# First loads and first products of a gated linear-attention and SwiGLU kernel: x tile 0 alone on one queue, x tile 1 on the other, two key products moved ahead of a transpose

## The chip, the cores and the metric

The kernel runs on one core of a Trainium2 chip. The time is device microseconds of one execution. Six runs of the kernel before gave a median of 179.36 us.

## The reference

All inputs are bf16. `x` is 2048 x 512, `wqkv` 512 x 1536, `wo` 512 x 512, `w1` and `w3` 512 x 1376, `w2` 1376 x 512, and `gate_w` has 512 entries. The attention has 32 heads of width 16.

```
qkv = x @ wqkv, split into q, k, v and 32 heads
phi(t) = where(t > 0, t + 1, exp(t)) + 1e-6
kv = sum over tokens of phi(k)^T v ;  z = sum over tokens of phi(k)
a = ((phi(q) kv) / (phi(q) . z + 1e-6)) @ wo
b = (silu(x @ w1) * (x @ w3)) @ w2
g = sigmoid(sum(x * gate_w))
out = g * a + (1 - g) * b
```

## The kernel before

**Tiles and stages.** The 2048 tokens are 16 tiles of 128 (`NT`), four tiles to a block of 512 (`NTB` = 4). The 512 features are four chunks of 128 (`KC`, index `kc`). The kernel has three stages. In the first it computes k for each token tile, applies phi, adds the results for z (`pks`, on GpSimd) and accumulates `XP`, which is x transposed times phi(k). In the second it turns `XP` into the matrix `W_sb`, while the gate and up products of the first block run. In the third it goes over the four blocks with the feed-forward products, the q products of the next block, and the output products. Everything is held in SBUF; each weight is loaded once.

**x in two layouts.** `XP` needs x with tokens on the partitions (`x_sb`). All other products need x with features on the partitions (`xT`). For tiles 2 to 15 `xT` comes by transposing DMAs (lines 87 and 91). For tiles 0 and 1 TensorE makes it: `emit_xT(t)` (line 170) issues four transposes of 128x128 from `x_sb` into two PSUM tiles `xTp`, two transposes to each. The first `xTp` (features 0 to 255, `kc` 0 and 1) is copied to `xT` by VectorE (line 180), the second (`kc` 2 and 3) by ScalarE (line 182). The two calls use four different PSUM buffers (tags XP0 to XP3).

**The loads and their queues.** Two engines issue DMAs: SyncE (queue SP, `dq` in the code) and, for one load only, ScalarE (queue ACT). Line 82 loads x tiles 0 and 1 together on SP; each partition takes two neighbouring tokens, which are 2 KB in one piece. Tile 0 is then the even tokens of the first 256 and tile 1 the odd ones, and the stores of output tiles 0 and 1 use the same pattern (`out_first`, lines 81 and 377). Line 83 loads the first half of the key weights (`wk_sb`, `kc` 0 and 1) on ACT, and line 84 the second half (`kc` 2 and 3) on SP. Behind them on SP come the transposing load of tiles 2 and 3 (line 87), the rest of x, and the other weights in the order of their use. The weights `w2` come in two halves (lines 110 and 111).

**The order on TensorE** is the program's own: `tc.manual_schedule` (line 151) fixes it, so that a matmul which waits holds up all that stands behind it. First come nine warm-up matmuls on constants (`emit_warm`, line 166: six of 512 columns, three of 128), which need no data. Then follow `emit_xT(0)`, `emit_xT(1)`, and the key products of lines 385 and 386: `kc` 0 and 1 of tile 0, `kc` 0 and 1 of tile 1, `kc` 2 and 3 of tile 0. Line 389 does the rest of tile 1, and then tiles 2 and 3. The key products `kc` 0 and 1 of a tile read the `xT` half that VectorE copied, and the first half of `wk_sb`. From tile 4 on, the key products (`k_ps`) alternate with the `XP` products (line 396).

**ScalarE at the start** issues the load of line 83, then loads the activation table and runs a one-element Exp (line 86), and is then free for the copies of line 182.

Of the kernel before, what the change touches and what calls it, by code (L numbers as in the profile page):

```python
# [17 lines left out]
def kernel(  # L18
# [12 lines left out]
    nc = tc.nc  # L31
    P = nc.NUM_PARTITIONS
# [7 lines left out]
    TB = 512  # L40
    NTB = S // TB
    TPB = TB // P
    FC = F // P
# [5 lines left out]
    x2d = A_x.flatten_outer_dims()  # L49
    out2d = out.flatten_outer_dims()  # L50
# [11 lines left out]
    x_sb = consts.tile([P, NT, D], BF16, name="x_sb")  # L62
# [7 lines left out]
    w2_sb = consts.tile([P, FC, D], BF16, name="w2_sb")  # L70
# [6 lines left out]
    x_r = x2d.rearrange("(t p) d -> p t d", p=P)  # L77
    dq = nc.sync
    TF = 2
    x_first = x2d[0 : TF * P, :].rearrange("(p j) d -> p j d", j=TF)  # L80
    out_first = out2d[0 : TF * P, :].rearrange("(p j) d -> j p d", j=TF)
    dq.dma_start(out=x_sb[:, 0:TF, :], in_=x_first)
    nc.scalar.dma_start(out=wk_sb[:, 0:2, :], in_=wqkv_r[:, 0:2, D : 2 * D])
    dq.dma_start(out=wk_sb[:, 2:4, :], in_=wqkv_r[:, 2:4, D : 2 * D])
    pre = consts.tile([1, 1], FP32, name="pre")
    nc.scalar.activation(out=pre[:], in_=nc.const_aps.tensor(0.0, [1, 1], FP32), func=ACT.Exp)
    dq.dma_start(
        out=xT[:, :, TF * P : TB], in_=x2d[TF * P : TB, :], transpose=True
    )
    for tb in range(1, NTB):  # L90
        dq.dma_start(
            out=xT[:, :, tb * TB : (tb + 1) * TB], in_=x2d[tb * TB : (tb + 1) * TB, :],
# [7 lines left out]
    with nc.allow_non_contiguous_dma(reason="one gate weight per partition and chunk"):  # L100
        dq.dma_start(
            out=wr_sb[:, :, 2 * FR : NR], in_=gate_w.rearrange("(kc d o) -> d kc o", d=P, o=1)
# [4 lines left out]
        dq.dma_start(out=w3_sb[:, :, fsl], in_=w3_r[:, :, fsl])  # L107
    dq.dma_start(out=wo_sb[:], in_=A_wo.rearrange("(kc d) n -> d kc n", d=P))
    w2_r = B_w2[0:FM, :].rearrange("(fc f) d -> f fc d", f=P)
    for fcs in (slice(0, FC // 2), slice(FC // 2, FC)):  # L110
        dq.dma_start(out=w2_sb[:, fcs, :], in_=w2_r[:, fcs, :])
    dq.dma_start(out=w2r_sb[:FR, :], in_=B_w2[FM:F, :])

    pk_sb = consts.tile([P, NT, D], BF16, name="pk_sb")
# [5 lines left out]
        out=bm, in_=bm, pattern=[[-Dh, HPC], [0, Dh]], compare_op=ALU.is_ge, fill=0.0,  # L120
# [3 lines left out]
        out=bm, in_=bm, pattern=[[Dh, HPC], [0, Dh]], compare_op=ALU.is_ge, fill=0.0,  # L124
# [34 lines left out]
    def emit_warm(*widths):  # L159
        warm = psX.tile([P, TB], FP32, tag="XP3", name="warm")  # L160
        for n in widths:
            nc.tensor.matmul(  # L162
                warm[:, 0:n], lhsT=warm_l, rhs=warm_r[:, 0:n], start=True, stop=True
            )

    emit_warm(TB, TB, TB, TB, TB, TB, P, P, P)

    st = {}

    def emit_xT(t):  # L170
        for h in range(2):
            xTp = psX.tile([P, 2, P], BF16, tag=f"XP{(2 * t + h) % 4}", name="xTp")
            for j in range(2):
                kc = 2 * h + j
                nc.tensor.transpose(  # L175
                    out=xTp[:, j, :], in_=x_sb[:, t, kc * P : (kc + 1) * P], identity=ident[:]
                )
            xT_t = xT[:, 2 * h : 2 * h + 2, t * P : (t + 1) * P]
            if h == 0:
                nc.vector.tensor_copy(out=xT_t, in_=xTp[:])  # L180
            else:
                nc.scalar.activation(out=xT_t, in_=xTp[:], func=ACT.Copy)

    def emit_k_mm(k_ps, t, kc):
        nc.tensor.matmul(  # L185
            k_ps[:], lhsT=xT[:, kc, t * P : (t + 1) * P], rhs=wk_sb[:, kc, :],
            start=(kc == 0), stop=(kc == KC - 1),
        )
# [148 lines left out]
    def emit_out(tb, tt):  # L337
        t = tb * TPB + tt
        tsl = slice(tt * P, (tt + 1) * P)

        if t < NT - 1:
            parts = [(0, D, True)]
        else:
            h, q7 = D // 2, 7 * D // 8
            parts = [(0, h, True), (h, q7, False), (q7, D, True)]
        if t < NT - 1:
            o_out = work.tile([P, D], BF16, tag="o_out", name="o_out")
        else:
            o_out = consts.tile([P, D], BF16, name="o_last")
        lo = 0  # L350
        for i, (a, b, store) in enumerate(parts):
            o_ps = psX.tile([P, b - a], FP32, tag=f"XP{2 + (tt + i) % 2}", name="o_ps")
            for c in range(KC):
                nc.tensor.matmul(  # L354
                    o_ps[:], lhsT=st[tb, "pqT"][:, c, tsl], rhs=W_sb[:, c, a:b],
                    start=(c == 0), stop=False,
                )
            nc.tensor.matmul(  # L358
                o_ps[:], lhsT=st[tb, "hTr"][:, tsl], rhs=w2r_sb[:, a:b],
                start=False, stop=False,  # L360
            )
            for fc in range(FC):
                nc.tensor.matmul(  # L363
                    o_ps[:], lhsT=st[tb, "hT"][:, fc, tsl], rhs=w2_sb[:, fc, a:b],
                    start=False, stop=(fc == FC - 1),
                )
            if i == 0:
                nc.scalar.activation(  # L368
                    out=o_out[:, a:b], in_=o_ps[:], func=ACT.Copy, scale=omg[:, t : t + 1]
                )  # L370
            else:
                nc.vector.tensor_scalar(  # L372
                    out=o_out[:, a:b], in0=o_ps[:], scalar1=omg[:, t : t + 1], scalar2=None,
                    op0=ALU.mult,
                )
            if store:
                rows = out_first[t] if t < TF else out2d[t * P : (t + 1) * P, :]
                nc.sync.dma_start(out=rows[:, lo:b], in_=o_out[:, lo:b])
                lo = b


    k0 = [psM.tile([P, D], FP32, tag="mm", name=f"k0_{t}") for t in range(TPB)]
    emit_xT(0)
    emit_xT(1)
    for kc, t in ((0, 0), (1, 0), (0, 1), (1, 1), (2, 0), (3, 0)):
        emit_k_mm(k0[t], t, kc)
    emit_k_phi(k0[0], 0)
    for t in range(1, TPB):
# [15 lines left out]
    with tc.manual_schedule(engines={ENG.DVE}):  # L404
# [18 lines left out]
        for dc in range(KC):  # L423
# [9 lines left out]
            out=z_sb[:].rearrange("p (b f) -> p b f", f=Q),  # L433
            in_=z_col[:, :, None].to_broadcast([P, NB, Q]),
        )
        kvT_ps = psX.tile([P, KC, P], FP32, tag="XP0", name="kvT_ps")
        for c in range(KC):
# [7 lines left out]
            out=kvT_sb[:], in0=kvT_ps[:],  # L445
# [22 lines left out]
    for tb in range(NTB):  # L468
        for fc in range(FC if tb == 0 else 0, FC):
            emit_ffn(tb, fc)  # L470
        nx = tb + 1
        for tt in range(TPB):
            if nx < NTB:
                emit_q(nx, tt, psX, "XP0")
                if tt % 2 == 0:
                    emit_rem(nx, tt // 2, psX, "XP1")
                    if tt == 2:
                        emit_omg(nx)
            emit_out(tb, tt)
            if nx < NTB:  # L480
                emit_den(nx, tt)
        if nx < NTB:
            emit_norm(nx)
# [30 lines left out]
```

## Time and profile before

| what | value |
|---|---|
| median of six runs (lowest, highest) | 179.36 us (178.57, 179.77) |
| the profiled execution, its own time | 179.77 us |
| its span, first to last instruction | 177.9 us |
| TensorE busy | 173.5 us, 98% of the span |
| VectorE, ScalarE, GpSimd busy | 119.1, 65.1, 63.8 us |
| x tiles 0 and 1 (256 KB): issued, time to landing | 0.81 us, 2.8 us |
| first half of wk (256 KB): issued, time to landing | 0.80 us, 3.5 us |
| second half of wk (256 KB): issued, time to landing | 1.27 us, 3.9 us |

All starts are counted from the first instruction of the span. The profiled execution is the longest of the six; 1.87 us of its time lie outside the span. A matmul's listed duration is longer than its distance to the next one, because matmuls overlap in the array; where the text speaks of the time that a matmul takes, it means the distance between starts.

### The profile page before, as it was taken

The numbers are of one execution on the slowest core, as the hardware profiler recorded it, in microseconds if no ns is written. First come the engines' busy times: TensorE is split into PE (matmuls) and PEld (weight loads), VectorE is DVE, ScalarE is ACT, GpSimd is POOL, SyncE is SP. The second block draws the span as 40 slices with busy tenths as digits, with TensorE's granted clock in tenths as the row PEclk, the third lists the DMA queues.
The fourth block names the chain that finished last, engine by engine and source line by source line (L and its number), as shares of the span: only waits on it lengthen the run. The fifth ranks groups of instructions, "written<-read, shape, count | busy, mean of one in ns | idle before, by whom it ended". The sixth has DMA issues, their size and how long they took to land.

```text
span 177.9 us, 2456 instructions
## 1 busy us (share of the span) xinstructions
PE 173.5 (98%) x867; PEld 84.2 (47%) x883; DVE 119.1 (67%) x205; ACT 65.1 (37%) x122; POOL 63.8 (36%) x80
## 2 busy tenths in 40 slices
PE   8999999999999999999999999999999999999993
PEld 4444444474444545444454544444545444444463
DVE  0398667899999837498786375978754669776001
ACT  3542423476532333342333333342433323331221
POOL 6087765689154323262003232620032328000000
PEclk9999999999999999999999999999999999999999
DMA  5999999901005011123000111240001012200002
GB/s 177 245 288 240 298 365 360 329 8 29 10 0 115 3 44 33 44 59 89 0 0 11 37 37 37 59 90 6 0 7 58 16 60 69 59 0 0 29 30 62
DMA packets 30252, 15.14 MB, mean 85 GB/s; under 512 B 20672, under 2 KB 30112, under 8 KB 30240
## 3 DMA queue, kind: packets, MB, share of 16 engines
q1 hardware_dynamic: 29968, 14.72, 30.2%
q10 hardware_dynamic: 272, 0.26, 0.5%
q8 instruction: 7, 0.11, 0.3%
q14 instruction: 5, 0.04, 0.1%
HBM read 8.42 MB, written 2.10 MB: 59 GB/s over the span
## 4 chain that ended last, share of the span: by engine, by line
PE 97%; issue 1%; DVE 0%
PE up_ps L321 19%; PE gate_ps L313 19%; PE o_ps L363 19%; PE XP L205 8%; PE o_ps L354 8%; PE q_ps L218 8%; PE k_ps L185 6%; PE r_ps L242 3%; PE k L185 2%; PE o_ps L358 2%; PE warm L162 2%; PE kvT_ps L440 1%; PE W_ps L458 0%; PE xTp L175 0%; DVE o_last L372 0%
## 5 line engine op out<-in xcount | busy, mean ns | idle before, releaser
L321 PE MATMUL up_ps<-xT,w_sb 128*128 128x512 bf16 x157 | 40.7, 379 | 0.2
L313 PE MATMUL gate_ps<-xT,w_sb 128*128 128x512 bf16 x157 | 40.7, 379 | 0.2
L226 POOL TENSOR_TENSOR qz<-pq,z_sb 128x512 f32<-128x512 bf16 x16 | 18.5, 1164 | 58.0 <-DVE pq L146 58.0
L326 ACT ACTIVATE th<-gate_ps 128x512 bf16<-128x512 f32 x40 | 23.9, 598 | 39.1 <-PE gate_ps L313 37.6
L363 PE MATMUL o_ps<-w_sb,hT 128*128 128x512 bf16 (+3 forms) x177 | 37.3, 355 | 0.2
L328 DVE SCALAR_TENSOR_TENSOR gs<-th,gate_ps 128x512 bf16<-128x512 bf16 x40 | 27.3, 682 | 5.4 <-ACT th L326 5.1
L333 DVE TENSOR_TENSOR hT<-up_ps,gs 128x512 bf16<-128x512 f32 x40 | 27.6, 691 | 3.8
L143 DVE TENSOR_SCALAR phi_m<-phi_e 128x512 bf16<-128x512 bf16 x32 | 13.6, 426 | 21.7 <-ACT phi_e L141 21.6
L363 PEld LDWEIGHTS <-hT 128*128 128x128 bf16 x180 | 16.9, 98 | 17.8
L321 PEld LDWEIGHTS <-w_sb 128*128 128x128 bf16 x160 | 15.7, 98 | 18.9
L313 PEld LDWEIGHTS <-w_sb 128*128 128x128 bf16 x160 | 15.6, 98 | 18.6
L293 POOL TENSOR_TENSOR pqn<-pq,rden 128x512 bf16<-128x512 bf16 x16 | 16.6, 1058 | 15.0 <-DVE rden L286 13.1
L368 ACT ACTIVATE o_out<-o_ps,omg 128x512 bf16<-128x512 f32 x15 | 10.3, 688 | 28.9 <-PE o_ps L363 28.9
L195 POOL TENSOR_TENSOR pks<-pks,pk_sb 128x512 f32<-128x512 f32 x15 | 17.4, 1162 | 7.3 <-DVE pk_sb L146 6.7
L354 PE MATMUL o_ps<-W_sb,pqT 128*128 128x512 bf16 (+3 forms) x70 | 16.7, 355 | 0.1
L205 PE MATMUL XP<-pk_sb,x_sb 128*128 128x512 bf16 x62 | 16.2, 379 | 0.1
L229 DVE TENSOR_REDUCE den<-qz 128x32 f32<-128x512 f32 x16 | 10.9, 684 | 7.9 <-POOL qz L226 7.8
L218 PE MATMUL q_ps<-wq_sb,xT 128*128 128x512 bf16 x61 | 16.1, 379 | 0.1
L141 ACT ACTIVATE phi_e<-k_ps 128x512 bf16<-128x512 f32 x12 | 7.2, 597 | 14.4 <-PE k_ps L185 14.4
L141 ACT ACTIVATE phi_e<-q_ps 128x512 bf16<-128x512 f32 x16 | 9.6, 597 | 7.8 <-PE q_ps L218 6.7
L185 PE MATMUL k_ps<-wk_sb,xT 128*128 128x512 bf16 x48 | 12.3, 379 | 0.0
L146 DVE SCALAR_TENSOR_TENSOR pq<-q_ps,phi_m 128x512 bf16<-128x512 f32 x16 | 11.1, 691 | 0.5
(60 smaller groups left out, 120.8 us busy)
## 6 DMA issues: line engine op xcount, KB each, us to landing
w_sb<-in_B_w_dram SPq DMA_DIRECT2D x6, 640.0 KB, 8.6
out_dram<-o_out SPq DMA_DIRECT2D x15, 128.0 KB, 1.9
x_sb<-in_A_x_dram SPq DMA_DIRECT2D x2, 512.0 KB, 4.2
x_sb<-in_A_x_dram SPq DMA_DIRECT2D x1, 768.0 KB, 5.1
wq_sb<-in_A_wqkv_dram SPq DMA_DIRECT2D x1, 512.0 KB, 4.9
wv_sb<-in_A_wqkv_dram SPq DMA_DIRECT2D x1, 512.0 KB, 6.4
wo_sb<-in_A_wo_dram SPq DMA_DIRECT2D x1, 512.0 KB, 10.2
wk_sb<-in_A_wqkv_dram ACTq DMA_DIRECT2D x1, 256.0 KB, 3.5
```

The costliest lines, as they stand in the source:

```text
L185: nc.tensor.matmul(k_ps[:], lhsT=xT[:, kc, t * P : (t + 1) * P], rhs=wk_sb[:, kc, :], start=(kc == 0), stop=(kc == KC - 1),)
L195: nc.gpsimd.tensor_add(pks[:], pks[:], pk_sb[:, t, :])
L205: nc.tensor.matmul(XP_ps[dc][:], lhsT=x_sb[:, t, dc * P : (dc + 1) * P], rhs=pk_sb[:, t, :], start=(t == 0), stop=(t == NT - 1),)
L218: nc.tensor.matmul(q_ps[:], lhsT=xT[:, kc, ts_tok], rhs=wq_sb[:, kc, :], start=(kc == 0), stop=(kc == KC - 1),)
L226: nc.gpsimd.tensor_tensor(out=qz[:], in0=st[tb, "pq"][:, tt, :], in1=z_sb[:], op=ALU.mult)
L313: nc.tensor.matmul(gate_ps[:], lhsT=w1_sb[:, kc, fsl], rhs=xT[:, kc, tok_sl], start=(kc == 0), stop=(kc == KC - 1),)
L321: nc.tensor.matmul(up_ps[:], lhsT=w3_sb[:, kc, fsl], rhs=xT[:, kc, tok_sl], start=(kc == 0), stop=(kc == KC - 1),)
L326: nc.scalar.activation(out=th[:], in_=gate_ps[:], func=ACT.Tanh, scale=0.5)
L328: nc.vector.scalar_tensor_tensor(out=gs[:], in0=th[:], scalar=1.0, in1=gate_ps[:], op0=ALU.add, op1=ALU.mult)
L333: nc.vector.tensor_tensor(out=st[tb, "hT"][:, fc, :], in0=up_ps[:], in1=gs[:], op=ALU.mult)
L354: nc.tensor.matmul(o_ps[:], lhsT=st[tb, "pqT"][:, c, tsl], rhs=W_sb[:, c, a:b], start=(c == 0), stop=False,)
L363: nc.tensor.matmul(o_ps[:], lhsT=st[tb, "hT"][:, fc, tsl], rhs=w2_sb[:, fc, a:b], start=False, stop=(fc == FC - 1),)
```

## The change

The load of x is split. Tile 0 goes first and alone on SP, in rows of 1 KB, with the plain token order. Tile 1 goes on ACT, behind the first half of wk. The stores of output tiles 0 and 1 use the plain order too. One of the six wide warm-up matmuls is taken out. The first two key products of tile 0 are issued between the transposes of tile 0 and those of tile 1. The two loads of `w2` become one.

```diff
-    x_first = x2d[0 : TF * P, :].rearrange("(p j) d -> p j d", j=TF)
-    out_first = out2d[0 : TF * P, :].rearrange("(p j) d -> j p d", j=TF)
-    dq.dma_start(out=x_sb[:, 0:TF, :], in_=x_first)
+    dq.dma_start(out=x_sb[:, 0, :], in_=x_r[:, 0, :])
     nc.scalar.dma_start(out=wk_sb[:, 0:2, :], in_=wqkv_r[:, 0:2, D : 2 * D])
+    nc.scalar.dma_start(out=x_sb[:, 1, :], in_=x_r[:, 1, :])
     dq.dma_start(out=wk_sb[:, 2:4, :], in_=wqkv_r[:, 2:4, D : 2 * D])
...
-    for fcs in (slice(0, FC // 2), slice(FC // 2, FC)):
-        dq.dma_start(out=w2_sb[:, fcs, :], in_=w2_r[:, fcs, :])
+    dq.dma_start(out=w2_sb[:], in_=w2_r)
...
-    emit_warm(TB, TB, TB, TB, TB, TB, P, P, P)
+    emit_warm(TB, TB, TB, TB, TB, P, P, P)
...
-                rows = out_first[t] if t < TF else out2d[t * P : (t + 1) * P, :]
+                rows = out2d[t * P : (t + 1) * P, :]
...
     emit_xT(0)
+    emit_k_mm(k0[0], 0, 0)
+    emit_k_mm(k0[0], 0, 1)
     emit_xT(1)
-    for kc, t in ((0, 0), (1, 0), (0, 1), (1, 1), (2, 0), (3, 0)):
+    for kc, t in ((0, 1), (1, 1), (2, 0), (3, 0)):
         emit_k_mm(k0[t], t, kc)
```

## The prediction, made before the changed kernel was run

> **What bounds the kernel now.** I read the page first, then the chain of work that ended last, the waits of TensorE, the order of time at the start, and the DMA queues in short stretches. The page and the waits of TensorE:
>
> ```profile
> span 177.9 us, 2456 instructions
> PE 173.5 (98%) x867; PEld 84.2 (47%) x883; DVE 119.1 (67%) x205; ACT 65.1 (37%) x122; POOL 63.8 (36%) x80
> PE 97%; issue 1%; DVE 0%
> ```
>
> ```profile
> PE warm L162 <- PEq L498: 0.8, 1, 0.8
> ```
>
> TensorE waits once, for 0.8 us, before its first instruction, and never again. So a delay of TensorE near the start has no later wait to vanish in: it reaches the end in full, and so does a gain. All that matters of this change is what it does to TensorE's stream in the first 7 us. The chain there (start, duration, what):
>
> ```profile
> 0.84 3.04 PE warm L162 x9
> 3.88 0.85 PE xTp L175 x8
> 4.74 4.43 PE k L185 x16
> 9.17 0.86 PE XP L205 x4
> ```
>
> and the same stretch in order of time (start, duration, engine, line):
>
> ```profile
> 3.63 0.84 PEld L175 LDWEIGHTS <-x_sb 128*128 128x128 bf16 x8
> 3.68 1.06 PE L175 MATMUL xTp<-ident,x_sb 128*128 128x128 bf16 x8
> 4.13 0.72 DVE L180 COPY xT<-xTp 128x256 bf16<-128x256 bf16 x2 [4.13 <-PE xTp L175]
> 4.35 0.81 ACT L182 ACTIVATE xT<-xTp 128x256 bf16<-128x256 bf16 x2 [1.56 <-PE xTp L175]
> 4.48 0.20 PEld L185 LDWEIGHTS <-xT 128*128 128x128 bf16 x2
> 4.53 2.91 PE L185 MATMUL k<-wk_sb,xT 128*128 128x512 bf16 x8
> ...
> 5.39 0.15 PEld L185 LDWEIGHTS <-xT 128*128 128x128 bf16 x1 [0.28 <-issue]
> 5.81 0.15 PEld L185 LDWEIGHTS <-xT 128*128 128x128 bf16 x1 [0.28 <-issue]
> ```
>
> Three things are to be seen. First, the **pace**: key weights load at 5.39 and 5.81, so a 512-column matmul takes 0.43 us here, while four of them take 0.86 us (0.216 each) from 9.17 on. The 16 key products last from 4.53 to the XP start at 9.01, 4.48 us: n x 0.427 + (16 - n) x 0.216 = 4.48 gives n = 4.9, so the pace doubles near 4.53 + 4.9 x 0.427 = 6.6 us. Second, the **latency of a transpose**: the first starts at 3.68, VectorE starts its copy at 4.13 and ends it at 4.42 (one copy is 0.29), and the first key weights load at 4.48, so a key product can start 0.85 us after the first transpose of its tile. Four transposes take 0.43 us (0.85 / 8 x 4). The transposes of tile 1 fill exactly the other 0.42 us. Third, x lands at 0.81 + 2.8 = 3.61, just as the warm-up ends.
>
> **What the Trainium skill says.** "TensorE: Matmul & The Clock Gate", Part 1: the array starts at half clock, and a free-running window of about 3.4 us decides; a window busy enough gives the full clock. The trace agrees on the halving (0.427 and 0.216 us). With TensorE busy from 0.84 and the change of pace at 6.6, 5.8 us later, it fits a window that began near 3.2, the one before it (-0.2 to 3.2) having been busy for 69% only ((3.2 - 0.84) / 3.41). How busy is enough, no run here shows. Part 4 of the page says that transposes don't count as busy in the same way; the trace neither shows nor excludes it. "DMA: Bandwidth & Descriptors", section "Issuing engines are not separate DMA queues": loads of both queues share the same 16 engines and interleave. The trace agrees: in the stretch from 2.6 to 3.5 us both queues moved packets (q1 is SP, q10 is ACT; packets, MB, share).
>
> ```profile
> q10 hardware_dynamic: 173, 0.18, 65.7%
> q1 hardware_dynamic: 74, 0.12, 34.8%
> ```
>
> **The change part by part.** Times are for the profiled execution at the slow pace.
>
> One warm-up matmul less: -0.43 us, so tile 0's transposes can start at 3.68 - 0.43 = 3.25, if x tile 0 is there. Of the 256 KB of x, SP had moved 0.14 MB by 2.6 us, ahead of any packet of ACT. Tile 0 alone is 128 KB, so its last packet goes near 2.6 us. For wk's first half the last packets go near 3.95 and it lands at 4.30, 0.35 later; the same lag puts tile 0 at about 3.0. Bounds: 2.95, and 3.61 if smaller rows win nothing. I take no wait; the far bound costs 0.4.
>
> First key products straight behind tile 0's transposes: their copy is no longer covered. Transposes 3.25 to 3.68, first product at 3.25 + 0.85 = 4.10: a **new wait of 0.42**. The product needs wk's first half too. That landed at 4.30 before; it is now without the second half of x beside it, but wk's second half can move up on SP. Bounds 3.7 and 4.45, I take 4.1 and a wait of 0.05 more (0 to 0.4).
>
> Tile 1's transposes behind these two products: 4.15 + 2 x 0.43 = 5.0. They need x tile 1, which queues behind wk's first half on ACT. Before, 768 KB (x, both halves of wk) had landed by 1.27 + 3.9 = 5.17; now the same bytes hold tile 1, ahead of that end or at it. Bounds 4.6 and 5.2; I take 5.1, a wait of 0.1 (0 to 0.2). The next instruction in the fixed order is tile 1's first key product, which waits for tile 1's copy: a **second new wait of 0.42**. Queued behind it are all further matmuls, those of tile 0 with `kc` 2 and 3 among them, which would be ready.
>
> Sum at the slow pace: -0.43 + 0.42 + 0.05 + 0.10 + 0.42 = +0.56. If the pace doubles at the same moment as before and after all of this, as at 6.6 us in the profiled execution, 0.56 us of slow work is made up in half the time, +0.28. If it doubles ahead of tile 1's first product, nearly all stays. The moment is free-running, so over the executions I take +0.45, between the two.
>
> Parts at nothing. ACT issues one DMA more, past which the table load and the small Exp move: about 0.46 us (the first issue's duration), so the Exp, which ended at 2.79, ends at 2.79 + 0.46 = 3.25; the ScalarE copy that it could hold up is due at 3.25 + (4.35 - 3.68) = 3.92, and 0.67 us cover it. SP issues the same number of loads ahead of the transposing load of tiles 2 and 3, in 0.40 and 0.41 us; that one lands at 1.73 + 4.3 = 6.0 and its first product starts near 7.3 (the ninth of the 16); it would have to lose 1.3 us to matter. One load of w2 for two: issued from 24.5 to 28.3, landing in 10.7 us, read first at 59.6; its cover is over 20 us, and the next SP work after these loads is at 40.1. GpSimd's queue gets nothing. Stores of output tiles 0 and 1: the same bytes in the same 1 KB rows, 15 stores of 1.9 us, none at the end of the chain.
>
> **The unknown: the clock.** The two waits put 0.84 us of idleness into the 3.4 us that decide: a window that holds both is 75% busy instead of 100%, and with one 88%. Known so far is only that 69% didn't suffice. If 75% or less suffices, nothing happens; if not, such a window fails and the next decides, 3.41 us later, at half speed: 3.41 / 2 = 1.7 us lost. A gain is excluded, since nothing here makes TensorE busier. For the forecast I allow for a late window in one execution in ten, +0.15.
>
> **Forecast**: +0.45 + 0.15 = +0.6. The profiled execution would go from 179.77 to 180.37; it lies 0.41 above the median, and the shift is applied to the median: 179.36 + 0.6 = 180.0.
>
> **Rivals.**
> *Late clock in most executions.* For it: the waits stand where the deciding window stood (3.2 to 6.6). Against it: a low threshold would explain the trace too. +0.45 + 1.7 = +2.15, 181.5.
> *The load isn't faster.* Tile 0 lands at 3.6 after all, and the removed warm-up becomes a wait: the sum without 0.43, times the same share (0.45 / 0.56), 0.99 x 0.8 = +0.8, and with +0.15, 180.3. Against it: the 0.14 MB by 2.6 us. This is also the case in which the change doesn't do what it says.
> *Faster.* The profile shows x landing 0.02 us ahead of its use. If in most executions it lands 0.8 us later than here, TensorE waits that long for it before the change, and not after it, since half the bytes still come in time: +0.45 - 0.8 = -0.35, 179.0. It decides from a lateness of about 0.5 us on. Against it: the one execution profiled is the slowest of the six and has no such wait.
>
> **How the numbers follow.** A measurement of this kernel can tell about 0.3% (0.54 us) from no change: 178.82 to 179.90. Forecast 57%, of which its +0.28 to +0.75 puts 31 above 179.90 and 26 within; late clock 25%, all slower; load not faster 8%, 6 slower and 2 within; faster rival 10%, 7 faster and 3 within. Sums: faster 7, within 31, slower 62. The range 179.2 to 181.8 leaves out most of the faster rival and the upper part of the late clock (up to 182.1 with the far bounds of the loads), some 2 in 10.
>
> **What would show it.** TensorE's waits: two new entries at the key products, one for each `xT` copy, of 0.4 us at the slow pace. The transposes fall in two groups of four, near 3.25 and 5.0. The weights of x tile 0 load at 3.2 and not at 3.6. The 16 key products and the doubled pace tell the clock: at 6.6 plus or minus a phase, or 3.4 us later. The prediction is wrong if the waits at the key products are below 0.2 us each, if x tile 1 lands after 5.3, or if the XP products begin ahead of 9.0 us.

## The result, and the profile after

| | before | changed |
|---|---|---|
| median (lowest, highest), executions | 179.09 us (178.55, 179.79), 42 | 179.91 us (179.50, 182.38), 20 |
| ratio to before, 95% interval | | 1.0078 [1.0057, 1.0100] |
| the profiled execution, its span | 179.77, 177.9 us | 179.78, 178.1 us |

The change makes the kernel slower, by 0.82 us in the medians. The ratio is larger than that of the medians, because the executions fall into **two groups** with nothing between them:

```
changed: 179.50 179.54 179.71 179.72 179.72 179.76 179.78 179.78 179.79 179.85 179.97
         181.51 181.56 181.67 181.76 181.78 181.83 181.89 181.92 182.38
```

Eleven lie around 179.76 (the median of that group), nine around 181.78. Before, all 42 lie between 178.55 and 179.79. The ratios here leave out single executions more than 1.5% above a kernel's fastest (182.38 above, and one each of the runs e1 and e10 below); the counts of late executions below hold all.

The profiled execution belongs to the lower group. From its page, and from its waits of TensorE (who waited for what: us in total, times, longest):

```profile
span 178.1 us, 2454 instructions
PE 172.8 (97%) x866; PEld 83.4 (47%) x882; DVE 119.1 (67%) x205; ACT 65.1 (37%) x122; POOL 63.8 (36%) x80
PE 94%; DMA 2%; issue 1%; DVE 1%; ACTq 0%
```

```profile
PE warm L160 <- PEq L498: 0.8, 1, 0.8
PE k L183 <- DVE xT L178: 0.4, 2, 0.3
PE xTp L173 <- DMA x_sb<-in_A_x_dram: 0.2, 1, 0.2
```

Where one wait of TensorE was listed, there are four, a DMA has come into the chain of work that ended last, and VectorE's share of it has grown from 0 to 1%. The wait for tile 0 isn't even among them: the times in this view are counted to the modelled end of the matmul ahead, which is later than the end of its place in the stream; the order of time shows the waits in full:

```profile
3.59 0.34 PEld L173 LDWEIGHTS <-x_sb 128*128 128x128 bf16 x4 [0.41 <-DMA x_sb<-in_A_x_dram]
3.60 0.61 PE L173 MATMUL xTp<-ident,x_sb 128*128 128x128 bf16 x4
4.03 0.29 DVE L178 COPY xT<-xTp 128x256 bf16<-128x256 bf16 x1 [4.03 <-PE xTp L173]
...
4.37 0.13 PEld L183 LDWEIGHTS <-xT 128*128 128x128 bf16 x2 [0.44 <-DVE xT L178]
4.38 0.84 PE L183 MATMUL k<-wk_sb,xT 128*128 128x512 bf16 x2 [0.17 <-DVE xT L178]
5.46 0.23 PEld L173 LDWEIGHTS <-x_sb 128*128 128x128 bf16 x4 [0.95 <-DMA x_sb<-in_A_x_dram]
5.46 0.40 PE L173 MATMUL xTp<-ident,x_sb 128*128 128x128 bf16 x4 [0.24 <-DMA x_sb<-in_A_x_dram]
...
6.13 0.39 PE L183 MATMUL k<-wk_sb,xT 128*128 128x512 bf16 x1 [0.28 <-DVE xT L178]
```

Tile 0's transposes could start at 3.25 and start at 3.60 (0.35). Four of them take 0.43 us, and the first product starts at 4.38 instead of 4.03 (0.35). Two products take 0.85 at the slow pace, and tile 1's transposes start at 5.46 instead of 5.23 (0.23). These four are already at the doubled pace (their weights load in 0.23 us, those of tile 0 in 0.34), so they take 0.22, and tile 1's first product starts at 6.13 instead of 5.68 (0.45). Counted so, the sum is 1.38 us of idleness in a stretch of 3 us in which before had none. It is in truth somewhat more: the second of the two products lasted 0.44 us where the first lasted 0.61, so the pace had doubled during it, and TensorE stood for about 0.4 us ahead of tile 1 and not 0.23. The gain is the one warm-up, 0.43.

The two profiled executions have nearly the same time, 179.77 and 179.78, and must not be compared by it: in the one of before the pace doubled at 6.6 us, in this one at 4.9 (most of the traces also record when TensorE's granted clock, the speed that the chip allows it, changes). Each us at the slow pace costs half a us, so the moment of doubling, which differs from execution to execution, is worth as much as the change: (6.59 - 4.90) / 2 = 0.85 us. Only the groups of executions tell the change's worth.

The loads explain two of the waits (KB, us from issue to landing):

```profile
wk_sb<-in_A_wqkv_dram ACTq DMA_DIRECT2D x1, 256.0 KB, 3.4
wk_sb<-in_A_wqkv_dram SPq DMA_DIRECT2D x1, 256.0 KB, 4.1
x_sb<-in_A_x_dram SPq DMA_DIRECT2D x1, 128.0 KB, 2.7
x_sb<-in_A_x_dram ACTq DMA_DIRECT2D x1, 128.0 KB, 4.1
```

Tile 0 lands at 0.81 + 2.7 = 3.5, a tenth ahead of the 256 KB of before, and tile 1 at 1.29 + 4.1 = 5.4. The DMA queues of the changed kernel show what held them up (packets, MB, share; the stretches are 1.8 to 2.5, 2.5 to 3.3 and 4.1 to 4.9 us; q1 is SP, q10 ACT):

```profile
q1 hardware_dynamic: 116, 0.11, 92.3%
q10 hardware_dynamic: 12, 0.01, 6.4%
...
q10 hardware_dynamic: 192, 0.19, 75.3%
q1 hardware_dynamic: 39, 0.03, 15.7%
...
q1 hardware_dynamic: 445, 0.15, 99.7%
q10 hardware_dynamic: 108, 0.09, 34.5%
```

By 2.5 us 0.11 MB of tile 0's 0.13 had started (the 116 packets count the small ones that signal completion). Then the queue of ACT took most of the engines, and SP's last packets of tile 0 came through among 192 of the key weights; the last of them started at 3.17. From 4.1 on it is the other way round: tile 1 on ACT shares the engines with the end of the key weights and the small packets of the transposing loads on SP, 445 against 108.

### The profile page after: what moved, and what is told of

Same layout as the page of the kernel before. It is cut to its first block, busy times and chain, and to the rows that moved or that the text cites. A ratio compares the mean times of both kernels' runs of the same rounds, so it can differ in the third digit from the quotient of the medians.

```text
span 178.1 us, 2454 instructions
## 1 busy us (share of the span) xinstructions
PE 172.8 (97%) x866; PEld 83.4 (47%) x882; DVE 119.1 (67%) x205; ACT 65.1 (37%) x122; POOL 63.8 (36%) x80
## 4 chain that ended last, share of the span: by engine, by line
PE 94%; DMA 2%; issue 1%; DVE 1%; ACTq 0%
PE up_ps L319 19%; PE gate_ps L311 19%; PE o_ps L361 19%; PE XP L203 8%; PE o_ps L352 8%; PE q_ps L216 8%; PE k_ps L183 6%; PE r_ps L240 3%; DMA x_sb<-in_A_x_dram 2%; PE o_ps L356 2%; PE k L183 2%; PE kvT_ps L440 1%; PE W_ps L458 0%; DVE o_last L370 0%; ACTq L81 0%
```

## The experiments

The first four take the change apart: the order alone, the loads alone, the idleness filled, and idleness alone.

**The order alone (e1).** Kernel before, with

```diff
     emit_xT(0)
+    emit_k_mm(k0[0], 0, 0)
+    emit_k_mm(k0[0], 0, 1)
     emit_xT(1)
-    for kc, t in ((0, 0), (1, 0), (0, 1), (1, 1), (2, 0), (3, 0)):
+    for kc, t in ((0, 1), (1, 1), (2, 0), (3, 0)):
```

> Kernel before with its own loads and six wide warm-ups; only the order is changed (two key products of tile 0 ahead of tile 1's transposes). Theory (two exposed copies plus the clock's window): first key product near 4.53 as before, tile 1's transposes near 5.4, its first key product near 6.25, two waits of about 0.4 us; a group of executions at about 179.1 + 0.6 = 179.7 us, and a second group about 2 us above it in some 4 of 10 executions, because the idle 0.85 us spoils a window. Rival (the upper group comes from x tile 1 landing late on ACT's queue): one group only, near 179.7, none above 181.

Measured: 179.67 us, ratio 1.0027 [1.0014, 1.0040]; 21 of 22 executions between 179.19 and 180.06, one at 182.02. Its TensorE in order of time:

```profile
3.68 0.63 PE L175 MATMUL xTp<-ident,x_sb 128*128 128x128 bf16 x4
4.48 1.03 PE L185 MATMUL k<-wk_sb,xT 128*128 128x512 bf16 x2 [0.17 <-DVE xT L180]
5.30 0.63 PE L175 MATMUL xTp<-ident,x_sb 128*128 128x128 bf16 x4
6.11 3.43 PE L185 MATMUL k<-wk_sb,xT 128*128 128x512 bf16 x14 [0.17 <-DVE xT L180]
```

The two copy waits are there, 4.48 - (3.68 + 0.43) = 0.37 and 6.11 - (5.30 + 0.43) = 0.38 us. Their cost, about 0.5 us, is as expected. The upper group is not: with 0.75 us of idleness, one execution in 22 is late (here and below: above 180.9 us), where 4 in 10 were expected. So the theory was right on the waits and wrong on how little idleness it takes. The rival, that the upper group comes from x tile 1 landing late, did better here; e3, e4 and e10 below decide between the two.

**The loads alone (e2).** The changed kernel with the old order put back (the diff above, reversed).

> Changed kernel with the old order (both tiles' transposes first); the split loads and the five wide warm-ups stay. Theory: x tile 1 lands near 5.4 as in the changed kernel, TensorE stands from about 4.0 to 5.4, then needs no further wait for copies; +0.7 to +1.4 us against before, 179.8 to 180.5 in the lower group, and with 1.4 us of idleness in one piece the upper group (near 182) holds half of the executions or more. Rival (the moved key products are what costs): 179.1 or below.

Measured: 181.53 us, ratio 1.0124 [1.0079, 1.0168]; six executions, two near 180.0 and four at 181.5 to 182.4. TensorE waits for x tile 1 in one piece:

```profile
5.76 0.40 PE L173 MATMUL xTp<-ident,x_sb 128*128 128x128 bf16 x4 [1.88 <-DMA x_sb<-in_A_x_dram]
```

Behind tile 0's transposes (3.25 + 0.43 = 3.68) that is 2.08 us. The moved products are not what costs most: with these loads they cover part of the wait for tile 1.

**Idleness filled (e3, and again as e10).** The changed kernel, with work on constants in each wait. e10 has 384 columns where e3 has two times 128 ahead of `emit_xT(1)`.

```diff
+    emit_warm(P)
     emit_xT(0)
+    emit_warm(384)
     emit_k_mm(k0[0], 0, 0)
     emit_k_mm(k0[0], 0, 1)
+    emit_warm(P, P)
     emit_xT(1)
+    nc.tensor.matmul(k0[3][:, 0:384], lhsT=warm_l, rhs=warm_r[:, 0:384], start=True, stop=True)
```

> Changed kernel plus warm-up matmuls on constants in each wait: 128 columns ahead of tile 0's transposes, 384 behind them, 2 x 128 ahead of tile 1's transposes, 384 behind them. No data comes earlier, TensorE only stays busy. Theory of the clock's window: the lower group stays near 179.75 us, the upper group (181.5 to 181.9 in the changed kernel) is gone, median 179.7. Rival (the upper group has another cause, late loads or the lost warm-up): 4 of 10 executions stay near 181.7.

> All waits of the changed kernel filled with warm-ups again, now with 384 instead of 2 x 128 columns ahead of tile 1's transposes: mainly for the count of executions. Theory: no execution above 181, median 180.0 to 180.4 us, some tenths above the changed kernel's lower group because a filler that is still running holds up the transposes. Rival (another cause of the upper group): 4 in 10 above 181.

Measured: e3 180.22 us, 1.0067 [1.0043, 1.0090], six executions between 179.97 and 180.35, half a us above the 179.7 that was expected. e10 179.97 us, 1.0048 [1.0033, 1.0064]; 15 of 17 between 179.77 and 180.39, one at 181.16 and one at 182.55. Together 2 of 23 are late, against 9 of 20 without the fillers, though no datum comes earlier. The upper group thus hangs on TensorE being idle, not on when the loads land. Against the lower group (179.76) the fillers cost 0.2 to 0.5 us: where one of them is still running when the data is there, it delays the work. That two are late stays open; the profiled executions of both still have gaps, 0.74 us in e3 and 0.80 us in e10.

**Idleness alone (e4 and e11).** The kernel before, with four and with five wide warm-ups in place of six.

```diff
-    emit_warm(TB, TB, TB, TB, TB, TB, P, P, P)
+    emit_warm(TB, TB, TB, TB, P, P, P)
```

> Kernel before with four wide warm-ups instead of six; loads and order untouched. TensorE then stands about 0.85 us ahead of x's landing at 3.6, and nothing that needs data moves. Theory of the clock's window: a lower group like before, 178.6 to 179.8, and an upper group some 1.7 us above it in part of the executions. Rival (only waits for data cost time, the clock doesn't care for 0.85 us): as before, 179.1, no execution above 180.2.

> Kernel before with five wide warm-ups instead of six, nothing else: TensorE stands 0.3 to 0.5 us ahead of x's landing. Theory: too little idleness to lose a window; 178.6 to 179.9 us, median within 0.2 us of before. Rival (any gap ahead of the first real work makes the clock late): some executions above 180.5, as with four wide warm-ups (4 of 6).

Measured: e4 180.94 us, 1.0093 [1.0057, 1.0130]; two executions at 179.78, four from 180.93 to 181.74. e11 179.25 us, 1.0005 [0.9987, 1.0022], all 14 between 178.61 and 179.95. The profiled execution of e4:

```profile
3.79 1.03 PE L175 MATMUL xTp<-ident,x_sb 128*128 128x128 bf16 x8 [0.76 <-DMA x_sb<-in_A_x_dram]
4.62 4.62 PE L185 MATMUL k<-wk_sb,xT 128*128 128x512 bf16 x16
```

Without its wait the transposes of e4 would start at 3.68 - 2 x 0.427 = 2.83; they start at 3.79, 0.96 later, and yet only 0.11 later than those of before. This kernel loses 1.9 us in the median (before had 179.00 beside it) for 0.11 us of later data: dispensable work on constants is what kept the clock in time. In e11 the gap is 3.74 - 3.25 = 0.49 us, and costs nothing. The sixth wide warm-up as such is thus worth nothing, and its removal gains nothing either, while x lands at 3.6 to 3.7.

The next five ask which part of the change brings the late clock.

**The sixth warm-up put back (e5).**

> Changed kernel with the sixth wide warm-up put back. Theory (idleness of all waits together decides whether the clock comes late): the wait for x tile 0 goes, some 0.15 us less idleness; TensorE's real work starts at 3.68 again, +0.1 us at most; lower group 179.7 to 179.9, upper group rarer than in the changed kernel, about 3 in 10 instead of 4.5. Rival (the lost warm-up itself makes the clock late): no execution above 181.

Measured: 180.27 us, 1.0068 [1.0038, 1.0098]; seven of nine executions between 179.83 and 180.54 (their median, 180.15, is above the 179.7 to 179.9 expected), two at 182.06 and 182.30. The rate, 2 in 9, isn't told apart from 9 in 20, but the lost warm-up isn't the cause by itself. The profiled execution is a late one, which shows what "late" is. Its weight loads for the key products:

```profile
9.29 0.15 PEld L183 LDWEIGHTS <-xT 128*128 128x128 bf16 x1 [0.28 <-issue]
9.72 0.15 PEld L183 LDWEIGHTS <-xT 128*128 128x128 bf16 x1 [0.28 <-issue]
10.14 0.98 PEld L183 LDWEIGHTS <-xT 128*128 128x128 bf16 x5 [0.28 <-issue]
```

The loads are 0.43 us apart up to 10.14, and five fit into the next 0.98 us. The pace doubles near 10.2 us, where it was 6.6 in the profiled execution of before.

**x tile 1 on SP (e6).** The changed kernel with one line moved.

```diff
     dq.dma_start(out=x_sb[:, 0, :], in_=x_r[:, 0, :])
+    dq.dma_start(out=x_sb[:, 1, :], in_=x_r[:, 1, :])
     nc.scalar.dma_start(out=wk_sb[:, 0:2, :], in_=wqkv_r[:, 0:2, D : 2 * D])
-    nc.scalar.dma_start(out=x_sb[:, 1, :], in_=x_r[:, 1, :])
```

> Changed kernel with x tile 1 on SP right behind tile 0 and ahead of the second half of wk. Theory: tile 1 lands by about 4.1 us, well ahead of its transposes at 5.2, so the wait for it goes; what stays are the two copy waits and a short wait for tile 0; lower group 179.3 to 179.7 us, and at most 1 execution in 10 above 181, as with the order alone. Rival (the queue of x tile 1 doesn't matter): as the changed kernel, 4 in 10 above 181.

Measured: 179.55 us, 1.0022 [1.0010, 1.0034], all 22 executions between 178.95 and 180.31. The upper group is gone. Its TensorE:

```profile
3.40 0.61 PE L173 MATMUL xTp<-ident,x_sb 128*128 128x128 bf16 x4
4.17 1.03 PE L183 MATMUL k<-wk_sb,xT 128*128 128x512 bf16 x2 [0.17 <-DVE xT L178]
5.00 0.63 PE L173 MATMUL xTp<-ident,x_sb 128*128 128x128 bf16 x4
5.81 3.59 PE L183 MATMUL k<-wk_sb,xT 128*128 128x512 bf16 x14 [0.17 <-DVE xT L178]
```

Tile 1's transposes follow the products without a wait (4.17 + 0.85 = 5.02). What stays is 0.15 for tile 0 and 0.34 and 0.38 for the copies, 0.87 us. The place of tile 1 makes up most of the change's loss: 1.0078 behind 256 KB on ACT, 1.0022 behind 128 KB on SP. Whether it is the queue or the smaller load ahead of it, no run separates.

**The second copy covered (e7).**

```diff
-    for kc, t in ((0, 1), (1, 1), (2, 0), (3, 0)):
+    for kc, t in ((2, 0), (3, 0), (0, 1), (1, 1)):
```

> Changed kernel with tile 0's key products of chunks 2 and 3 moved ahead of tile 1's first key products, so that they cover tile 1's copy. Theory: the second copy wait (0.28 to 0.35 us) goes; lower group 179.4 to 179.5 us, and fewer late clocks than in the changed kernel, 1 to 3 in 10. Rival (the second half of wk is no earlier than the copy): same times as the changed kernel, 179.75, and as many above 181.

Measured: 180.25 us, 1.0076 [1.0050, 1.0103]; twelve of 19 executions between 179.47 and 180.59, seven from 181.29 to 182.15. In the profiled execution tile 1's transposes (5.45) are followed by products at 5.68, without a wait. But the wait for the tile itself stays, and 7 in 19 are late, not the 1 to 3 in 10 expected; the lower group didn't become faster either (its median is 179.78). The expectation failed, and covering the copy alone doesn't help.

**Both tiles on SP, and the old order (e8).** e6 with the old order.

> x tiles 0 and 1 in two loads, both on SP, five wide warm-ups, and the order of before: the split without its queue and without the moved products. Theory: tile 0 lands near 3.3 to 3.5, tile 1 near 3.8 to 4.1, transposes follow each other with at most 0.2 us of waits, the first key product starts 0.1 to 0.3 us ahead of before: 178.9 to 179.1 us, no execution above 180.2. Rival (any split of x costs): 179.3 or more.

Measured: 179.62 us, 1.0023 [1.0004, 1.0043]; 13 of 14 between 178.92 and 180.09, one at 181.17. Tile 1 as the second load on SP is later than expected, and its transposes start at 4.49, 0.76 behind tile 0's (3.30 + 0.43):

```profile
4.49 0.40 PE L173 MATMUL xTp<-ident,x_sb 128*128 128x128 bf16 x4 [0.58 <-DMA x_sb<-in_A_x_dram]
```

The rival held: a split of x costs in each form that was tried. With both tiles on SP the order makes no difference (e6 1.0022, e8 1.0023).

**Only the wait for x tile 1 filled (e9).** The changed kernel with `emit_warm(TB)` ahead of `emit_xT(1)`.

> Changed kernel with one 512-column warm-up ahead of tile 1's transposes, in the wait for x tile 1 (0.24 to 0.7 us in the profiles so far) and nowhere else. Theory (the idleness adds up, and the wait for x tile 1 puts it over the edge): 0.4 us less idleness brings it to that of the moved order alone; at most 1 execution in 10 above 181, lower group 179.7 to 180.0 us. Rival (the two copy waits or the lost warm-up make the clock late): 4 in 10 above 181 as before this edit.

Measured: 180.02 us, 1.0062 [1.0038, 1.0086]; 16 of 21 between 179.71 and 180.33, five from 181.77 to 182.33. It lies between the theory and its rival. Its profiled execution, a late one, has waits of 0.25 for tile 0 (3.50 instead of 3.25), 0.35 and 0.38 for the copies, 0.98 us in sum.

**One load of w2 (e12).** Kernel before with this line of the change alone.

> Kernel before with the one load of w2 in place of two, nothing else. Theory: nothing, 179.0 to 179.3 us, the load lands more than 20 us ahead of its first use. Rival (the longer issue holds up what follows on SP): 0.3 us or more.

Measured: 179.11 us, 1.0000 [0.9985, 1.0016]. Nothing, as expected.

**All runs together.** I add up, for one profiled execution each, how much later TensorE's matmuls start than the stream ahead of them would allow. Kernels with up to some 0.9 us of idleness (e1 0.75, e6 0.87, e11 0.49, e3 0.74, e10 0.80) have 3 late executions in 81 (1 of 22, 0 of 22, 0 of 14, 0 of 6, 2 of 17). Those with more (the changed kernel 1.38, e9 0.98, e7 0.92, e5 1.36, e4 0.96, e2 2.08) have 9 of 20, 5 of 21, 7 of 19, 2 of 9, 4 of 6 and 4 of 6, which is 31 in 81. The profiled executions of e5 and e9 are late ones themselves. e8 doesn't fit well: 0.76 us ahead of tile 1, and a further wait for tile 2 behind it, with one of 14 late. A profiled execution is one of many, and the loads land differently in each; the border at 0.9 is no sharper than that.

The record of the granted clock says more than the sum. In the traces that have it, TensorE is at the doubled pace for 170.67 or 174.08 us, which is 50 or 51 times 3.413 us. This fits a clock that is decided on in windows of 3.41 us, one behind the other, each ending where the clock can change. The table has the share of each window in which matmuls or transposes stream (from their starts, 0.427 us for 512 columns at the slow pace), up to the window at whose end the pace doubles:

| profiled execution | pace doubles at | busy in the window that ends there | in the windows ahead of it, nearest first |
|---|---|---|---|
| before | 6.59 us | 100% | 68% |
| changed | 4.90 us | 79% | 19% |
| e2 | 3.97 us | 83% | 0% |
| e4 | 6.64 us | 84% | 58% |
| e5 (late) | 10.16 us | 100% | 58%, 73% |
| e8 | 4.39 us | 78% | 4% |
| e9 (late) | 10.18 us | 100% | 72%, 70% |

e3, e7, e10 and e12 lie between these (82 to 100%; ahead, at most 56%); e1, e6 and e11 have no record. Each window that brought the doubling was busy for 78% or more, each one that didn't for 73% or less. (If the windows end 0.2 us ahead of the recorded change, it is 78% and 69%.) So it is idleness within one window that counts, about a quarter of it, and not the sum: the window of the changed kernel's profiled execution closed at 4.90, ahead of the waits for tile 1. Transposes count as busy here: without them, the windows of e8 and of the changed kernel would have passed with 66%, while one of e5 without any transpose failed with 73%. An estimate from these figures: of all positions in which windows can lie over the changed kernel's waits, with a border of 73 to 78%, a third to somewhat over half come late. Nine in 20 executions did. For e6 the same estimate gives none at 73% and a quarter at 75%; with 0 of 22 seen, the border is likely near its lower end.

## Why the prediction was right, and where it was off

**No later wait takes the delay up.** Right: behind 9 us the changed kernel's TensorE has no wait that the one before had not, and e12 shows the one load of w2 to be free. The plain order of the two output stores was not run alone.

**Two new copy waits of 0.42.** Right in place and nearly in size: 0.35 and 0.45 in the changed kernel, 0.37 and 0.38 in e1, 0.34 and 0.38 in e6. e1 prices them at +0.27% [0.14, 0.40], 0.5 us, between +0.42 and +0.84, what the two waits are worth ahead of the doubling (half) and behind it (in full). The wait of 0.05 for the key weights did not come.

**"I take no wait" for x tile 0.** This step failed, almost up to its far bound: the wait was 0.35 against 0.4, and the weights of tile 0 load at 3.59, where the prediction had named 3.6 as the sign against it. The estimate took the last packet of 128 KB to go near 2.6 us and added the lag of another load, 0.35. The lag was about right. But the last packets come through only beside ACT's load, the last at 3.17, and the tile lands at 3.5. Halving the bytes gained 0.1 us of landing time, so the removed warm-up mostly became a wait. That was the rival "the load isn't faster", and it is true as a part of the result.

**0.1 for x tile 1.** Mis-sized in the same direction: 0.23 to 0.4 in the profiled execution of the changed kernel and 5.97 - (4.48 + 0.85) = 0.64 in that of e5. The tile landed at 5.4, and the prediction had named "after 5.3" as a sign that it is wrong. The bound of 5.2 rested on the bytes that had landed by 5.17 before. It left out that SP goes on to its transposing loads while ACT still holds tile 1. In both kernels the first of their packets starts at 4.24 us. Before, only the end of the key weights was still to come then (last packet 4.57); in the changed kernel it was most of tile 1 (last packet near 4.9). How much of the delay this sharing makes, no run separates. The wait for tile 1 is the term that matters most: e6 takes it away and the late clock with it.

**The sum without the clock.** +0.45 was forecast; the lower group moved by 179.76 - 179.09 = +0.67 us. The two load terms are enough for the difference, though the lower group is a selection: it leaves out the executions that came late.

**The clock.** The mechanism was right, the share wrong. One late execution in ten was allowed for; 9 in 20 came. The prediction counted 0.84 us of idleness, 75% busy in a window that holds both waits, and gave a late clock in most executions 25%. Those two waits alone stay just on the safe side: e1 has one late execution in 22. The waits for the two loads, which the sum had at 0 and 0.10, took the changed kernel over the border. The size was near: the upper group lies 2.0 us above the lower, against 1.7 from half of a window. That idleness decides, and not late data, is shown by e4 (idleness without later data: 4 of 6 late) and by e3 and e10 (later data without idleness: 2 of 23 late). That it is a share of a window of about 3.4 us, as the Trainium skill ("TensorE: Matmul & The Clock Gate", Part 1) has it, agrees with the recorded clock: multiples of 3.413 us, and a border between 73 and 78%. The late pace of e5 comes 3.6 us after that of before. But one execution of each kernel is recorded, and nobody chose where its windows lie; that their place decides which executions are late is an inference.

**How near 180.0 came.** That the measured median is 179.91 is in part luck. The forecast stood on 179.36, the median of six runs, and 42 runs gave 179.09. The forecast median moved by +0.6 and the measured one by +0.82, but only because 11 of 20 executions lie in the lower group: the ratio of 1.0078 is +1.4 us, more than twice the forecast. The mis-sized share of late executions accounts for most of that.

**The faster rival** had nothing for it: none of the 20 executions lies below 179.50, and before's loads land at 2.8 to 2.9 us in all profiled runs that keep them.

## What to carry to other kernels

Work that fills the time of a copy or a landing is worth keeping in its place: moving two products ahead of four transposes uncovered two copies of 0.35 us each and, with the loads as they were, gained nothing in exchange (e1). While TensorE is still at its slow pace, count idleness twice, as time lost and as a share of the window that decides on the clock: here kernels with gaps of about 0.9 us or more in the first 7 us had the doubling late (10.2 us in the two profiles of late executions, against 6.6 in that of before) in over a third of the executions, mostly some 2 us each, and work on constants was enough to prevent most of it. When executions fall into groups, read the groups; one profile of each kernel would have shown no difference here.

## What the runs showed of the hardware that was not expected

- Half the bytes don't land earlier in proportion: 256 KB of x in 2 KB rows took 2.8 to 2.9 us from issue to landing, 128 KB in 1 KB rows 2.4 to 2.7 us (the changed kernel, e2, e3, e5, e7, e9, e10). In the changed kernel 1.0 of the 2.7 us passed before the first packet of the 128 KB started (1.83), and about 0.4 after the last one did (3.17).
- The same 128 KB cost far more as the second load of ACT's queue than as the second of SP's, although each queue had issued only one load before it (256 KB on ACT, 128 KB on SP): it landed at 5.4 us or later, where e6's and e8's was there in time for transposes at 5.00 and 4.49.
- TensorE's doubled pace lasted 50 or 51 times 3.413 us in every trace that records it. It came where the 3.41 us ahead of it were busy for 78% or more, and not at the ends of earlier windows that were busy for 73% or less. Transposes counted as busy.
- The pace of TensorE doubled between 4.0 (e2) and 10.2 us (e5, e9) after the first instruction, in kernels whose first matmul always started at 0.84 us.
